# Projected tiles stored through two pairs of buffers in turn, and the upper halves of the last two tiles gated after the third product from the end

## The chip, the core and the metric

The kernel runs on one core of one Trainium2 chip. The core has a matrix engine (PE), a vector engine (DVE), a scalar engine (ACT), a general engine (POOL) and an engine that here issues all the transfers (SP). Each engine runs its own queue of instructions in order and waits on semaphores where it needs what another one makes. The metric is the device time of one execution in microseconds, as the median of several runs.

## The reference

Two branches are computed from the same normalised input, `x` of 2048 positions by 640 features, and multiplied: a dilated sliding window attention (32 heads, 8 places back in steps of 2) with an output projection `wo`, and a bilinear gated unit of 1536 hidden features.

```python
xn = _layernorm(x, axis=-1)
s = _A_ref(xn, A_wqkv, A_wo)                                  # attention(xn) @ wo
g = _silu(_B_ref(xn, B_w_gate, B_w_up, B_w_down))             # ((xn @ w_gate) * (xn @ w_up)) @ w_down
return x + s * g
```

## The kernel before

The 2048 positions are cut into 16 tiles of 128 (`NT`). All numbers are float32; a product is made of three passes of split operands: each operand is written as a high part (rounded, by ACT, the first line of `split`, L85) and a low part (the rest, by DVE or POOL, L86), and `mm3` (L95) adds high by high, high by low and low by high.

The stages follow one another as they are written, since the schedule is by hand: each engine gets its instructions in the order of the program text.

1. Normalisation, the projections to queries, keys and values, and the attention itself, whose vector work is woven in between the products of the gated unit's first half (`gate_up`). `gate_up` makes one chunk of the hidden layer for 512 positions at a time; its result stands in a tile of the pool tag `hs` and is stored to DRAM as `h_scr` (L404). There are 48 such tiles. A scratch tile of tag `gs` holds the gate half (L389), and POOL multiplies the two in the last chunks (L403). Both tags have two buffers, taken in turn.
2. The output projection, a loop over the tiles `s` from 0 to 15 (L766). In each round: `trans_o(s + 1)` transposes the next tile of attention output on DVE (L459) and splits it (L85 on ACT, L86 on DVE); `sum_wd` adds up parts of the down projection's weights on DVE (L507 to L513) from a loaded `wraw` tile; `out_proj(s)` makes two halves of 15 products each on PE into the PSUM tag `q` (4 buffers), evicts each half on ACT into a tile `y` of tag `gs` (L476) and stores `y` to DRAM as `s_scr` (L477); `split_wd` splits the weights (L85 on ACT, L86 on POOL). Tile 14's two split operands are themselves tiles of tag `hs` (L462), since their own tag is by then in use for the next stage.
3. The down projection, in Strassen's manner: 56 products (`n_prod`) of 18 matmuls each (L598), seven for every two tiles. `gather` collects them: of a pair of tiles a and b, the fourth product of the seven completes a's upper half (columns 320 on; L614), the fifth b's upper half (L618), the sixth a's lower half (L621) and the seventh b's lower half; each is then put through silu on ACT (L579). `gated` multiplies by the projected tile (L584), adds the input (L585) and stores to the output (L586); it takes a whole tile or one half. The projected tile and the input are loaded by `load_sx` (L569, L570) into tiles of tags `hs` and `gs`.

Transfers are issued by SP in program order. In the loop over products a pair of tiles is gated in the next pair's first two rounds; only the last pair, tiles 14 and 15, is gated at the end, in the round of product 54 (`m == n_prod - 2`) and after the loop.

Of the kernel before, what the change touches and what calls it, by code (L numbers as in the profile page):

```python
# [19 lines left out]
P = 128  # L20
S, D, F = 2048, 640, 1536
H, DH = 32, 20
W, DIL = 8, 2
NT = S // P
# [6 lines left out]
HALF = D // 2  # L31
# [13 lines left out]
def tile_column(s):  # L45

    return DIL * (s % NE) + s // NE
# [3 lines left out]
def kernel(  # L51
# [23 lines left out]
    def st(shape, tag, bufs, dt=F32):  # L75
        cnt[0] += 1
        return sb.tile(shape, dt, tag=tag, bufs=bufs, name=f"{tag}_{cnt[0]}")

    def pt(shape, tag, bufs):
        cnt[0] += 1  # L80
        return ps.tile(shape, F32, tag=tag, bufs=bufs, name=f"{tag}_{cnt[0]}")
# [8 lines left out]
    def mm3(acc, pairs, parts=ALL3, first=True, last=True):  # L90

        pairs = list(pairs)
        runs = [(a[i], b[j]) for i, j in parts for a, b in pairs]
        for n, (a, b) in enumerate(runs):
            nc.tensor.matmul(acc, a, b, start=first and n == 0, stop=last and n == len(runs) - 1)  # L95
# [372 lines left out]

    def out_proj(s):
        a = oT.pop(s)  # L470
        y = st([P, D], "gs", 2)
        for n in range(2):
            c = slice(n * HALF, (n + 1) * HALF)
            p = pt([P, HALF], "q", 4)
            mm3(p, [([t[:, k, :] for t in a], [t[:, c] for t in wo_s[k]]) for k in range(KD)])
            nc.scalar.activation(y[:, c], p, AF.Copy)  # L476
        nc.sync.dma_start(s_scr[s], y)  # L477
# [60 lines left out]
    def sum_h(m):  # L538

        n, name = m // 7, H_IN[m % 7]  # L540
        v = h_raw[n]
        if name == "S1":
            y = st([P, 2, KH, P], "wqh", 1)
            v["S1"], v["S2"] = y[:, 0], y[:, 1]
            nc.vector.tensor_add(v["S1"], v["A21"], v["A22"])
        elif name == "S2":
            nc.vector.tensor_sub(v["S2"], v["S1"], v["A11"])
        elif name == "S4":
            v["S4"] = st([P, KH, P], "wql", 1)
            nc.vector.tensor_sub(v["S4"], v["A12"], v["S2"])  # L550
        elif name == "S3":
            v["S3"] = v["A21"]
            nc.vector.tensor_sub(v["S3"], v["A11"], v["A21"])

    def hi_h(m):
        hT[m] = st([P, 2, KH, P], "wf", 4, F32R)
        nc.scalar.activation(hT[m][:, 0], h_raw[m // 7][H_IN[m % 7]], AF.Copy)

    def lo_h(m):
        n, name = m // 7, H_IN[m % 7]  # L560
        nc.vector.tensor_sub(hT[m][:, 1], h_raw[n][name], hT[m][:, 0].bitcast(F32))
        if name == "A22" and n + 2 < NT // 2:
            load_h(n + 2)
# [3 lines left out]
    def load_sx(s):  # L567
        a, b = st([P, D], "hs", 2), st([P, D], "gs", 2)
        nc.sync.dma_start(a, s_scr[s])  # L569
        nc.sync.dma_start(b, xv[:, tile_column(s), :])  # L570
        sx_t[s] = a, b
# [9 lines left out]
    def gated(s, half=None):  # L581
        c = slice(0, D) if half is None else slice(half, half + HALF)
        (a, b), y = sx_t[s], g_t[s]
        nc.vector.tensor_mul(y[:, c], y[:, c], a[:, c])  # L584
        nc.vector.tensor_add(y[:, c], y[:, c], b[:, c])  # L585
        nc.sync.dma_start(ov[:, tile_column(s), c], y[:, c])  # L586

    def product(m):
        j = m % 7
        name = W_IN[j]  # L590
        place = "ACACABA"[j]
        new = j in (0, 1, 5)
        if new:
            bank[place] = pt([P, HALF], {"A": "q", "B": "g", "C": "u"}[place], {"A": 4, "B": 2, "C": 2}[place])
        p, y = bank[place], hT.pop(m)
        runs = [(i, l, k) for i, l in ((0, 0), (0, 1), (1, 0)) for k in range(KH)]
        for r, (i, l, k) in enumerate(runs):
            nc.tensor.matmul(p, y[:, i, k], wd_t[name][k][:, l], start=new and r == 0, stop=r == len(runs) - 1,  # L598
                             skip_group_check=True)

    def gather(m):

        n, j = divmod(m, 7)
        a, b = 2 * n, 2 * n + 1
        p = bank["ACACABA"[j]]
        if j == 0:
            keep("M1", p, "lg", 2)
        elif j == 1:
            keep("M5", p, "lg", 2)
        elif j == 2:  # L610
            keep("U2", p, "e", 1)
        elif j == 3:
            g_t[a] = st([P, D], "q", 2)
            nc.vector.tensor_add(g_t[a][:, HALF:], kept["U2"], p)  # L614
            return lambda: silu(a, 1)
        elif j == 4:
            g_t[b] = st([P, D], "q", 2)
            nc.vector.tensor_add(g_t[b][:, HALF:], kept["M5"], p)  # L618
            return lambda: silu(b, 1)
        elif j == 5:  # L620
            nc.vector.tensor_add(g_t[a][:, :HALF], kept["M1"], p)  # L621
            return lambda: silu(a, 0)
        else:
            return lambda: silu(b, 0, p)
        return lambda: None
# [139 lines left out]
    n_prod = 7 * NT // 2  # L765
    for s in range(NT):  # L766
        k, part = divmod(s - 1, 2)
        if s == 1:
            begin_wd()
        if s + 1 < NT:  # L770
            trans_o(s + 1)
        if s in o_next:
            load_o(*o_next[s], st([P, o_next[s][1], D], "t", 2))
        if 0 <= k < KH:
            sum_wd(k, part)
        out_proj(s)
        if 0 <= k < KH:
            split_wd(k, part)
            if part and k + 2 < KH:
                load_wd(k + 2)  # L780
        if s == 12:
            load_h(0)
        if s == 14:
            hi_h(0)
            lo_h(0)
# [9 lines left out]
    for m in range(n_prod):  # L795
        n, j = divmod(m, 7)
        product(m)
        after = gather(m)
        if m + AHEAD < n_prod:
            hi_h(m + AHEAD)  # L800
        after()
        if m + AHEAD + 1 < n_prod:
            sum_h(m + AHEAD + 1)
        if m + AHEAD < n_prod:
            lo_h(m + AHEAD)
        if j < 2 and n:
            gated(2 * n - 2 + j)
            load_sx(2 * n + j)
        if m == n_prod - 2:
            gated(NT - 2)  # L810
            gated(NT - 1, HALF)
    gated(NT - 1, 0)


# [41 lines left out]
```

## Time and profile before

| what | value |
|---|---|
| median of 3 runs | 789.18 us (789.11 to 789.18) |
| profiled execution, its own time | 789.2 us |
| its span, first to last instruction | 787.3 us |
| granted PE clock | 0.999 |
| s_scr stores, issue to landing (min, median, max) | 2.1, 3.6, 8.0 us |
| out stores, issue to landing (min, median, max) | 1.8, 2.4, 4.5 us |

The profile is of one execution. The span is what the hardware profiler recorded on the core, and 1.9 us of the execution's time lie around it. Busy times are sums over an engine's instructions; matmuls overlap, so a row of 15 may be longer than its share of the time. In the waits a row reads: the engine and line that waited, the one that ended the wait, microseconds in total, times, longest. In the timeline a row reads: start, duration, engine, line, operation, what is written and read, and in brackets the idle time before it with what ended it. The chain of waits is followed back from the last instruction, and gives start, duration and engine of each piece.

### The profile page before, as it was taken

The page shows a single profiled execution, that of the slowest core. Times are in us where ns is not written, and L with a number is a line of the kernel's source. Part 1 is how long each engine was busy: PE and PEld are TensorE (multiplying, and loading weights), DVE is VectorE, ACT ScalarE, POOL GpSimd, SP SyncE. Part 2 cuts the span into 40 slices and gives each one's busy share as a digit, 9 for nine tenths or more (in the row PEclk, how much of TensorE's full clock was granted, in tenths as well). Part 3 has the DMA queues.
Part 4 walks back from the last instruction along what each step waited for, and adds up shares of the span by engine and source line. Part 5 has one row for each costly group of instructions (what it writes and reads, how often), then busy time and mean ns, then how long its engine had stood idle before and what let it go on. Part 6 is the DMA issues. An engine that isn't in the chain of part 4 may idle for free. (4 is left out here: it accounts for less than half of the span.)

```text
span 787.3 us, 11221 instructions
## 1 busy us (share of the span) xinstructions
PE 778.0 (99%) x4456; PEld 708.8 (90%) x4456; DVE 658.7 (84%) x658; ACT 234.6 (30%) x536; POOL 147.8 (19%) x110
## 2 busy tenths in 40 slices
PE   8999999999999999999999999999999999999997
PEld 6989898889898888898898989888899999999997
DVE  6889899999999979997999999991277677777775
ACT  5324211121112211311221212113356554444442
POOL 6201212022013200500231000113377600000000
PEclk9999999999999999999999999999999999999999
DMA  8272122141132321404032222322796574555533
GB/s 315 73 229 81 36 69 64 48 123 48 49 94 80 94 71 61 118 27 112 28 118 72 62 82 72 107 87 66 182 258 201 181 262 133 204 200 186 181 101 135
DMA packets 81517, 92.68 MB, mean 118 GB/s; under 512 B 23016, under 2 KB 63032, under 8 KB 81336
## 3 DMA queue, kind: packets, MB, share of 16 engines
q1 hardware_dynamic: 81464, 91.96, 37.7%
q8 instruction: 35, 0.57, 0.3%
q14 instruction: 18, 0.15, 0.1%
HBM read 54.53 MB, written 28.31 MB: 105 GB/s over the span
## 5 line engine op out<-in xcount | busy, mean ns | idle before, releaser
L95 PE MATMUL u<-xc,wf 128*128 128x512 f32 (+1 forms) x735 | 176.2, 390 | 0.0
L95 PE MATMUL g<-xc,wf 128*128 128x512 f32 (+1 forms) x735 | 176.1, 390 | 0.0
L95 PEld LDWEIGHTS u<-xc,wf 128*128 128x128 f32 x735 | 135.7, 187 | 32.2
L95 PEld LDWEIGHTS g<-xc,wf 128*128 128x128 f32 x735 | 135.3, 187 | 31.0
L95 PE MATMUL q<-wqh,xc 128*128 128x300 f32 (+1 forms) x960 | 159.7, 309 | 1.8 <-ACT xc L224 1.0
L95 PEld LDWEIGHTS q<-wqh,xc 128*128 128x128 f32 x960 | 146.0, 188 | 4.3 <-ACT xc L224 1.9
L321 DVE TENSOR_TENSOR t<-q,kv 128x1600 f32<-128x1600 f32 (+1 forms) x48 | 99.3, 2069 | 9.6 <-DMA kv<-kv 9.6
L342 DVE TENSOR_TENSOR t<-e,kv 128x1600 f32<-128x1600 f32 (+1 forms) x48 | 97.5, 2051 | 1.1
L86 POOL TENSOR_TENSOR wf<-wraw,wf 128x256 fp32r<-128x256 f32 (+2 forms) x22 | 47.8, 2197 | 247.6 <-ACT wf L85 229.3
L324 DVE TENSOR_REDUCE lg<-t 128x80 f32<-128x1600 f32 (+1 forms) x48 | 92.6, 1930 | 1.2
L389 ACT ACTIVATE gs<-g 128x512 f32<-128x512 f32 x48 | 28.7, 598 | 205.9 <-PE g L95 197.1
L95 PE MATMUL q<-wql,xc 128*128 128x300 f32 (+1 forms) x480 | 86.0, 309 | 0.0
L350 DVE TENSOR_TENSOR t<-t,t 128x1600 f32<-128x1600 f32 (+1 forms) x36 | 78.0, 2166 | 1.1
L95 PEld LDWEIGHTS q<-wql,xc 128*128 128x128 f32 x480 | 74.3, 188 | 0.0
L289 ACT ACTIVATE kv<-q 128x200 f32<-128x200 f32 (+1 forms) x96 | 33.5, 349 | 133.5 <-PE q L95 133.5
L598 PE MATMUL q<-xc,wf 128*128 128x320 f32 x432 | 67.3, 309 | 0.0
L598 PEld LDWEIGHTS q<-xc,wf 128*128 128x128 f32 x432 | 64.3, 188 | 0.0
L86 POOL TENSOR_TENSOR wql<-wraw,wqh 128x300 fp32r<-128x300 f32 (+4 forms) x15 | 34.2, 2300 | 142.6 <-ACT wqh L85 142.6
L95 PE MATMUL q<-wf,wf 128*128 128x320 f32 x156 | 35.9, 312 | 0.6 <-ACT wf L85 0.6
L400 DVE TENSOR_TENSOR hs<-u,gs 128x512 f32<-128x512 f32 x39 | 26.6, 683 | 0.8 <-issue 0.8
L95 PEld LDWEIGHTS q<-wf,wf 128*128 128x128 f32 x156 | 26.0, 188 | 0.9 <-ACT wf L85 0.8
L86 DVE TENSOR_TENSOR wf<-ot,wf 128x640 fp32r<-128x640 f32 x13 | 13.6, 1045 | 14.1 <-ACT wf L85 14.1
(160 smaller groups left out, 891.4 us busy)
## 6 DMA issues: line engine op xcount, KB each, us to landing
h_scr<-hs SPq DMA_DIRECT2D x48, 256.0 KB, 2.3
wraw<-in_wgu SPq DMA_DIRECT2D x12, 640.0 KB, 4.8
t<-h_scr SPq DMA_DIRECT2D x8, 768.0 KB, 7.4
s_scr<-gs SPq DMA_DIRECT2D x16, 320.0 KB, 3.6
hs<-s_scr SPq DMA_DIRECT2D x16, 320.0 KB, 4.4
gs<-in_x SPq DMA_DIRECT2D x16, 320.0 KB, 4.7
out<-q SPq DMA_DIRECT2D x15, 320.0 KB, 2.5
wraw<-h_scr SPq DMA_DIRECT2D x12, 384.0 KB, 5.7
```

Source lines behind the costliest of these rows:

```text
L86: eng.tensor_sub(lo, raw, hi.bitcast(F32))
L95: nc.tensor.matmul(acc, a, b, start=first and n == 0, stop=last and n == len(runs) - 1)
L289: nc.scalar.activation(kv_t[u][:, :, W - 1 + i, :], p[:, c:].rearrange("p (a c) -> p a c", a=2), AF.Copy)
L321: nc.vector.tensor_mul(t, q.rearrange("p i c -> p (i c)").unsqueeze(1).to_broadcast([P, 2, NE * c]), places(0, j))
L324: nc.vector.tensor_reduce(out=lg[:, :, j:j + 2].rearrange("p n a -> p a n"), in_=heads(t), op=ALU.add, axis=AX.X)
L342: nc.vector.tensor_mul(heads(t), pw, heads(places(1, j)))
L350: nc.vector.tensor_add(acc, acc, t)
L389: nc.scalar.activation(gs, pp[0], AF.Copy)
L400: nc.vector.tensor_mul(hs, pp[1], gs)
L598: nc.tensor.matmul(p, y[:, i, k], wd_t[name][k][:, l], start=new and r == 0, stop=r == len(runs) - 1, skip_group_check=True)
```

## The change

In `out_proj` the tile `y` is taken from tag `hs` for odd tiles 1 to 11, and from `gs` for all the others. In the last rounds of the loop over products, the gating of tiles 14 and 15 is ordered anew: after product 53 the upper halves of both, after product 54 the lower half of tile 14, and after product 55, as before, the lower half of tile 15. Tile 14 is thus gated and stored in two halves and not at once.

```diff
     def out_proj(s):
         a = oT.pop(s)
-        y = st([P, D], "gs", 2)
+        y = st([P, D], "hs" if s % 2 and s < NT - 4 else "gs", 2)
         for n in range(2):
...
         if j < 2 and n:
             gated(2 * n - 2 + j)
             load_sx(2 * n + j)
-        if m == n_prod - 2:
-            gated(NT - 2)
+        if m == n_prod - 3:
+            gated(NT - 2, HALF)
             gated(NT - 1, HALF)
+        elif m == n_prod - 2:
+            gated(NT - 2, 0)
     gated(NT - 1, 0)
```

## The prediction

> **What bounds the kernel now.** I read the busy times, then the waits between the engines, then the timeline wherever TensorE (PE) is not continuous.
>
> ```profile
> span 787.3 us, 11221 instructions
> PE 778.0 (99%) x4456; PEld 708.8 (90%) x4456; DVE 658.7 (84%) x658; ACT 234.6 (30%) x536; POOL 147.8 (19%) x110
> ```
>
> PE is busy for all but 9.3 us, so only a hole in PE, or what runs after the last product, can be won. The change touches two stretches: the output projection (562.8 to 634.5 us: 16 tiles of 30 products, 4.42 us a tile) and the last three products. The waits from 562 to 636 (total, times, longest, us) hold one long wait on ACT and one on PE:
>
> ```profile
> ACT gs L476 <- DMA s_scr<-gs: 3.4, 1, 3.4
> PE q L95 <- ACT wf L85: 0.6, 1, 0.6
> ```
>
> The timeline (start, duration, engine, line) says how they hang together:
>
> ```profile
> 569.25 9.16 SPq L477 DMA_DIRECT2D s_scr<-gs  x3
> 573.22 0.73 ACT L85 ACTIVATE wf<-ot 128x640 fp32r<-128x640 f32 x1
> 577.31 0.77 ACT L476 ACTIVATE gs<-q 128x320 f32<-128x320 f32 x2 [3.36 <-DMA s_scr<-gs]
> 579.40 0.74 ACT L85 ACTIVATE wf<-ot 128x640 fp32r<-128x640 f32 x1
> ...
> 585.65 0.46 PE L95 MATMUL q<-wf,wf 128*128 128x320 f32 x2
> 589.23 0.31 PE L95 MATMUL q<-q,wf 128*128 128x320 f32 x1
> 590.09 0.56 PE L95 MATMUL q<-wf,wf 128*128 128x320 f32 x2 [0.55 <-ACT wf L85]
> ```
>
> Tile 2's eviction (L476) stands at the head of ACT until tile 0's store has left the shared buffer: that store, issued at 569.25, takes 8.0 us to land (landing times by issue window). Every split behind it on ACT (L85) is late, DVE's lower part of tile 4 (L86) waits 2.86 us, and the lag reaches PE at tile 6 through the chain of waits:
>
> ```profile
> 586.20 1.16 DVE wraw L512
> 587.36 1.09 DVE e L513
> 588.45 0.77 DVE ot L459
> 589.30 0.75 ACT wf L85
> 590.09 44.39 PE q L95 x300
> ```
>
> From 590.09 to the last product PE never stops, so what the hole costs is paid at the end in full. The last rows are:
>
> ```profile
> 779.65 0.49 DVE L621 TENSOR_TENSOR q<-lg,g 128x320 f32<-128x320 f32 x1 [2.04 <-PE g L598]
> 780.67 0.82 DVE L584 TENSOR_TENSOR q<-q,hs 128x640 f32<-128x640 f32 x1 [0.54 <-ACT q L579]
> 782.27 0.48 DVE L584 TENSOR_TENSOR q<-q,hs 128x320 f32<-128x320 f32 x1
> 782.28 0.44 ACT L579 ACTIVATE q<-q 128x320 f32<-128x320 f32 x1 [1.64 <-PE q L598]
> 783.20 0.48 DVE L584 TENSOR_TENSOR q<-q,hs 128x320 f32<-128x320 f32 x1
> 784.24 0.33 SPq L586 DMA_DIRECT2D out<-q  x1
> ```
>
> The silu of tile 15's lower half is done at 782.72, but its multiply starts at 783.20: DVE is still busy with tile 15's upper half. DVE, not PE, is last there, by 0.48 us.
>
> **Part one: hs for odd tiles 1 to 11.** No instruction is added and none changes size; buffers and waits change.
> - Removed: tile 2's wait on tile 0's store. It now takes the other gs buffer, whose reader (POOL's L403) ended at 565.0. Tile 4, the next on tile 0's buffer, evicts after 582.6; the store landed at 577.3.
> - Added: tile 1 (evicts at 570.24) and tile 3 (about 578.6) wait for the stores of the last two hs tiles of the gate-and-up stage. These were issued at 558.04 and 566.06 and land after 2.5 and 8.8 us, at 560.5 and 574.9: cost nothing, with 9.7 and 3.7 us of cover. Queued behind tile 1's eviction on ACT are three wd splits and tile 3's split, for which POOL and PE wait; without that cover this is the last rival. Tiles 5 to 11 reuse a buffer four tiles on (17.6 us) against a longest landing of 8.0: nothing.
> - Added: the two hs operands of tile 14 wait for the stores of tiles 9 and 11. Tile 11's is issued by about 617.4 (its second eviction starts at 616.87), so lands at 621.0 by the median of 3.6, before DVE's row at 623.8. Even at 8.0 it lands at 625.4, the lower part is then ready at 626.3, and PE first needs it ten products into tile 14, at 627.0: nothing.
> - SP issues the same stores; tile 2's moves from 578.1 to about 576.6, and the wd and o loads behind it by as much.
>
> Then ACT runs on: tile 2's evictions at 574.0 and 576.2, four wd splits of 0.36 to 578.0, tile 4's split done at 578.7 (580.14 before; PE wants it at 580.4). For tile 5 DVE follows with L86 to 579.5, two wd sums at the slow 1.16, a transpose of 0.83, ACT 0.75: 583.2 against PE's 584.8. For tile 6, L86 to 584.7 (1.48, the slow row), two sums at 1.16, transpose and split: 588.6 against 589.2. So the hole should close. It is worth 590.09 - 589.23 - 0.147 (the usual pitch of products) = 0.71, plus 0.10 (the pair after it, 0.56 for 0.46), plus 0.07 (tile 5's first pair, at 584.85, took 0.53) = **0.88 us**. Bounds: 0, if the slow rows stack up; 0.9, as PE has no other hole here.
>
> **Part two: both upper halves after product 53.** Four DVE rows of 0.49 and two stores now stand ahead of L621. L618 ends at 777.61; tile 14's upper half runs to 778.6 and tile 15's to 779.56, while L621 cannot start before PE ends product 54 (779.65). Their operands are there: tile 15's silu at 778.16, its hs at 777.7, its gs at 773.83 + 4.7 = 778.5. Product 54 hides the 1.95 us; uncovered, they would push L621, which has 1.06 us of slack (below). After L621 come silu (to 780.65) and tile 14's lower half: 2 x 0.49 plus two starts, 781.7 (was 782.35). DVE is then idle until 782.74, two starts of 0.02 after the silu; 0.48 + 0.02 + 0.49 later, at 783.75, SP can issue the last store, not 784.24: **0.49 us**. The split costs DVE 2 x (2 x 0.49 - 0.82) = 0.32 us and SP one more issue of 0.33, all before 782. SP is free: its last earlier issue (773.83, 1.93 us) ends at 775.8, and the four stores go out at about 778.7, 779.6, 781.7 and 783.75, each when its add is done. The last store keeps its 160 KB and its landing, 2.2 us here; the second of the same size landed in 1.8.
>
> **Sum** against the profiled execution: 787.3 - 0.88 - 0.49 = 785.9 us of span, and 789.2 - 1.37 = 787.8 with the 1.9 us around it. The median of the runs is 789.18, so the forecast is the same there: **787.8 us**, 0.17% less. I call 0.2% (1.58 us, so 787.60) the bound, about what a measurement of this kernel can tell from no change.
>
> **The rivals.**
> *The last store is also rid of a fetch: 787.4.* One packet of the instruction queue is in flight around the last store:
>
> ```profile
> q14 instruction: 1, 0.01, 0.8%
> ```
>
> (window 782 to 787.3: packets, MB, share of 16 engines; 0.8% of 16 x 5.3 is 0.7 us on one DMA engine.) The rows of the store are all but through at 785.6, and single packets of one engine trickle to 786.0. That is the 2.2 against 1.8. If the store, half a microsecond earlier, gets clear of it, 0.4 more is won: -1.77. For: the fetch may hang on something that does not move with DVE. Against: it starts shortly after DVE's last row, and may be set off by it. The Trainium skill (DMA: Bandwidth & Descriptors, Queues, rings and completion order) says that a DMA engine takes turns between its queues packet by packet and that one queue is the runtime's own, which fits a single delayed engine; by that rule the sum would be 787.4 if the two miss each other and 787.8 if not.
>
> *The hole stays, only the end is won: 788.7* (789.2 - 0.49). Beside POOL a wd sum takes 1.16, alone 0.48:
>
> ```profile
> 574.99 1.16 DVE L512 TENSOR_TENSOR wraw<-wraw 128x320 f32<-128x320 f32 x1
> 594.74 0.48 DVE L512 TENSOR_TENSOR wraw<-wraw 128x320 f32<-128x320 f32 x1
> ```
>
> POOL also starts earlier, so the two may meet more. I have charged the slow figure throughout and still have 0.6 us at tile 6, so little speaks for it. The Trainium skill (SBUF — State Buffer, Who interferes with whom) has a DVE instruction with two SBUF inputs and a POOL instruction that reads SBUF block one another; if each of the three DVE rows ahead of tile 6 lost a whole POOL row of 1.1, not 0.7, tile 6 would be ready 1.2 us later and the time 788.3 to 788.7.
>
> *Only the hole closes, the end stays: 788.3* (789.2 - 0.88): gs of tile 15 lands over a microsecond later than its 778.5, and holds L621 behind the upper half. This point is past only if L621 starts later than 780.7 instead of 779.65.
>
> *Slower: tile 1 gets the hs buffer of the late store.* It decides if that store lands after 570.24; the one issued at 566.06 does, at 574.9. ACT would then stand for 4.7 us; evictions 0.8, three splits 1.1 and tile 3's split 0.7 put that at 577.5, where PE wants it at 576.0: 1.5 us of hole, a second of up to 1.0 at tile 4 or 5 through DVE, and the old 0.88 kept. With the end's 0.49 off, +1.0 to +2.0: 790.2 to 791.2. Against it: 48 hs tiles came before, an even number, so tile 1 follows the last but one, stored at 558.04.
>
> **How the numbers follow.** Forecast 0.50 (787.55 to 788.1 by itself), the fetch missed 0.34, only the end 0.06, only the hole 0.03, slower 0.07. Faster by over 0.2%: 0.34 and 0.04 from the forecast's lower edge, 0.38; within 0.2%: 0.55; slower: 0.07. The range from 787.2 to 788.9 holds all but the slower case and strays.
>
> **What would show it.** Right: no wait of L476 on s_scr; ACT's split of tile 4 ends near 578.7; no hole near 590, and PE's last product ends at 781.4; the last L584 follows its silu at once, and the last store goes out 1.4 us earlier, at 782.9. Wrong: L476 waiting on h_scr near 570; a new PE wait on L85; L621 starting well after its product; a last landing far from 2.2.

## The result and the profile after

| | before | changed |
|---|---|---|
| median of 14 runs each on one chip | 789.39 us | 787.71 us (787.34 to 788.20) |
| ratio, 95% interval | | 0.9978 (0.9969 to 0.9986) |
| span of the profiled execution | 787.3 us | 785.8 us |
| output projection, start of its first matmul to that of the first product after it | 71.53 us | 70.60 us |
| down projection, start of its first matmul to that of its last | 147.62 us | 147.62 us |
| last silu's start to the end of the span | 5.0 us | 4.2 us |

The forecast was 787.8 us, 1.37 us or 0.17% less than before. The change took off 1.68 us by the medians, 0.21% (0.22% by the ratio of the table). That is just past the bound of 0.2%, with an interval that lies on both sides of it.

The page of the changed kernel begins (span; busy time, share and instructions of each engine):

```profile
span 785.8 us, 11227 instructions
PE 778.8 (99%) x4456; PEld 709.7 (90%) x4456; DVE 659.0 (84%) x660; ACT 234.7 (30%) x536; POOL 147.3 (19%) x110
```

Two more DVE instructions stand there. PE is idle for 7.0 us in place of 9.3. The waits from 562 to 636 us (who, for whom, total, times, longest) have these rows for the evictions, and none for PE (one more of 1.2 us, for which no engine is named, stands in the profile of before as well):

```profile
ACT gs L476 <- PE q L95: 15.1, 11, 1.7
ACT hs L476 <- PE q L95: 8.6, 6, 1.6
```

The evictions of both tags now wait for PE alone, as they should: ACT is ahead. The 3.4 us behind a store are gone. ACT's timeline (start, duration, line; the four weight splits after the third row are left out) shows tile 2's evictions and tile 4's split, and the chain of waits what it does for PE:

```profile
573.65 0.74 ACT L85 ACTIVATE wf<-ot 128x640 fp32r<-128x640 f32 x1
574.33 0.44 ACT L476 ACTIVATE gs<-q 128x320 f32<-128x320 f32 x1
576.47 0.44 ACT L476 ACTIVATE gs<-q 128x320 f32<-128x320 f32 x1 [1.71 <-PE q L95]
578.25 0.73 ACT L85 ACTIVATE wf<-ot 128x640 fp32r<-128x640 f32 x1
```

```profile
563.20 70.60 PE q L95 x480
```

Before, the unbroken piece held 300 products from 590.09 on; now it holds all 480 matmuls of the stage. The split of tile 4 begins at 578.25, not at 579.40. Among the last rows of the timeline are:

```profile
777.77 5.68 SPq L586 DMA_DIRECT2D out<-q  x4
778.18 0.49 DVE L585 TENSOR_TENSOR q<-q,gs 128x320 f32<-128x320 f32 x1
778.97 0.49 DVE L621 TENSOR_TENSOR q<-lg,g 128x320 f32<-128x320 f32 x1 [0.30 <-PE g L598]
781.60 0.44 ACT L579 ACTIVATE q<-q 128x320 f32<-128x320 f32 x1 [1.64 <-PE q L598]
782.07 0.49 DVE L584 TENSOR_TENSOR q<-q,hs 128x320 f32<-128x320 f32 x1 [1.05 <-ACT q L579]
```

DVE is through with the upper halves at 778.67, waits 0.30 us for PE, and after that 1.05 us for the last silu. The last multiply starts 0.47 us after the silu's start; before it was 0.92 (783.20 against 782.28).

The stretches add up to the difference of the spans: 0.93 less in the output projection, 0.79 less at the end, and 0.25 more ahead of both, where nothing was changed (the first matmul of the output projection starts at 563.03, before at 562.78). That start lay between 562.5 and 563.5 in the eight profiles of this study, so it is scatter and no effect.

### The profile page after: what moved, and what is told of

Read it like the earlier page. It is cut to its first block, busy times and chain, and to the rows that moved or that the text cites. A ratio compares the mean times of both kernels' runs of the same rounds, so it can differ in the third digit from the quotient of the medians.

```text
span 785.8 us, 11227 instructions
## 1 busy us (share of the span) xinstructions
PE 778.8 (99%) x4456; PEld 709.7 (90%) x4456; DVE 659.0 (84%) x660; ACT 234.7 (30%) x536; POOL 147.3 (19%) x110
## 4 chain that ended last, share of the span: by engine, by line
PE 99%; DVE 0%; ACT 0%; issue 0%; POOL 0%; POOLq 0%
PE q L95 36%; PE u L95 21%; PE g L95 21%; PE q L598 11%; PE u L598 5%; PE g L598 3%; PE q L157 1%; PE q L223 1%; ACT xc L224 0%; PE q L240 0%; DVE xc L225 0%; DVE q L584 0%; DVE q L585 0%; ACT q L579 0%; POOL ident masks.py:199 0%
## 5 line engine op out<-in xcount | busy, mean ns | idle before, releaser
L321 DVE TENSOR_TENSOR t<-q,kv 128x1600 f32<-128x1600 f32 (+1 forms) x48 | 97.7, 2036 | 10.0 <-DMA kv<-kv 10.0
L350 DVE TENSOR_TENSOR t<-t,t 128x1600 f32<-128x1600 f32 (+1 forms) x36 | 80.3, 2231 | 1.1
```

What stands on the lines that cost most here:

```text
L321: nc.vector.tensor_mul(t, q.rearrange("p i c -> p (i c)").unsqueeze(1).to_broadcast([P, 2, NE * c]), places(0, j))
L350: nc.vector.tensor_add(acc, acc, t)
```

## The experiments

In the diffs below, the kernel changed from is named first. `HS` stands for `"hs" if s % 2 and s < NT - 4 else "gs"`. Times are medians of 11 runs; each comes with its ratio to the kernel before on the same chip, whose median was 789.09 for the first four and 789.15 for the last two.

**The second pair of buffers alone** (from the changed kernel):

```diff
-        if m == n_prod - 3:
-            gated(NT - 2, HALF)
+        if m == n_prod - 2:
+            gated(NT - 2)
             gated(NT - 1, HALF)
-        elif m == n_prod - 2:
-            gated(NT - 2, 0)
```

> The second pair of buffers alone; the end is as it was before. Theory (hole and end are separate terms that add): the hole near 590 closes, L476 waits for no s_scr store, the output projection's 480 products run from 71.7 us to about 70.8, and the time is 0.9 us below before (ratio 0.9989); the last store lands after 2.2 us as in the profile of before. Rival (the end alone carries the gain, and the earlier products only lengthen a wait there): 0 to 0.2 us below before, with the end longer than the 5.0 us it took from the last silu on. If the last store lands after 1.8 us here too, the 0.4 us between the two landings has nothing to do with the new order of the end.

Measured: 788.05 us, ratio 0.9988 (0.9979 to 0.9997), 1.04 us below before. The chain of waits, the timeline and the output stores in a window around the last ones (size, time to landing) read:

```profile
563.38 70.60 PE q L95 x480
```

```profile
781.79 0.44 ACT L579 ACTIVATE q<-q 128x320 f32<-128x320 f32 x1 [1.64 <-PE q L598]
782.71 0.48 DVE L584 TENSOR_TENSOR q<-q,hs 128x320 f32<-128x320 f32 x1
```

```profile
out<-q SPq DMA_DIRECT2D x2, 160.0 KB, 1.8
```

The hole is closed to the same length as in the changed kernel, and the last multiply is as late as before (0.92 us after the silu's start). The last store landed after 1.8 us with the old order, too, not after the expected 2.2, and from the last silu the end took 4.6 us, not 5.0.

**The new order of the end alone** (from the changed kernel):

```diff
-        y = st([P, D], HS, 2)
+        y = st([P, D], "gs", 2)
```

> The new order of the end alone; all projected tiles go through gs as before. Theory: tile 2's eviction again waits 3.4 us for tile 0's store, PE has its hole near 590, and the time is 0.5 us below before if the last store takes 2.2 us to land, 0.9 us if 1.8 us as in the profile of the changed kernel (ratio 0.9994 to 0.9989). Rival (the halves of tile 14 only add work): no change or up to 0.3 us above before, with L621 starting later than 0.1 us after its product.

Measured: 788.73 us, ratio 0.9997 (0.9988 to 1.0005), 0.36 us below before (the quotient of the two medians is 0.9995). By this interval alone it can't be told from no change; the trace shows what it did. Among its waits from 562 to 636 and its last rows are:

```profile
ACT gs L476 <- DMA s_scr<-gs: 3.2, 1, 3.2
PE q L95 <- ACT wf L85: 0.5, 1, 0.5
```

```profile
779.75 0.49 DVE L621 TENSOR_TENSOR q<-lg,g 128x320 f32<-128x320 f32 x1 [0.26 <-PE g L598]
782.39 0.44 ACT L579 ACTIVATE q<-q 128x320 f32<-128x320 f32 x1 [1.64 <-PE q L598]
782.86 0.49 DVE L584 TENSOR_TENSOR q<-q,hs 128x320 f32<-128x320 f32 x1 [1.05 <-ACT q L579]
```

The wait and the hole are back (output projection 71.47 us), and the end is that of the changed kernel, 4.2 us from the silu on. The two parts are separate terms: each stretch is as long as in the changed kernel when its own part is there, whether the other is or not. By the medians 1.04 and 0.36 make 1.40 us. One figure of the expectation was missed: the last store landed after 1.8 us, for which a gain of 0.9 us was expected, and it was 0.36. The 0.9 took the landing of 2.2 us in the one profile of before for the usual one, and in two other profiles with the old order the last store landed after 1.8.

**hs for tile 1 only** (from the changed kernel):

```diff
-        y = st([P, D], HS, 2)
+        y = st([P, D], "hs" if s == 1 else "gs", 2)
```

> As the changed kernel, but hs for tile 1 only, all other tiles in gs. Theory (only tile 2's wait on the one late store ever cost anything): the same time as the changed kernel within 0.2 us, no wait of L476 on a store, no hole of PE. Rival (later stores also hold evictions back, and the second pair is needed to the end): a wait of L476 on s_scr at a later tile, and 0.3 us or more above the changed kernel.

Measured: 787.75 us, ratio 0.9983 (0.9974 to 0.9992): within 0.1 us of the changed kernel. The evictions' waits, besides the same 1.2 us, are:

```profile
ACT gs L476 <- PE q L95: 23.1, 16, 1.7
ACT hs L476 <- PE q L95: 0.7, 1, 0.7
```

No store holds any of them back, and the 480 products again take 70.60 us. One borrowed buffer moves tile 2 off tile 0's, and no later reuse needs the second pair.

**The buffer of the late store** (from the changed kernel), the rival on the slower side:

```diff
-        y = st([P, D], HS, 2)
+        y = st([P, D], "hs" if (s % 2 or s == 0) and s < NT - 4 else "gs", 2)
```

> As the changed kernel, but tile 0 takes hs as well, so that tile 1 gets the hs buffer whose store was issued at 566 and landed only at 575. Theory (the last rival's mechanism, which the even number of earlier hs tiles kept away): tile 1's eviction stands from about 571 to 575, PE has a hole of 1.5 us at tile 3 and up to 1.2 more at tiles 4 and 5, and the time is 1.5 to 2.8 us above the changed kernel (789.2 to 790.5). Rival (the four q banks and the split operands already made carry PE over a wait of 4 us): under 0.5 us above it.

Measured: 790.72 us, ratio 1.0020 (1.0011 to 1.0029): slower than before, and 2.97 us above the kernel with hs for tile 1 only, taken on the same chip. Among the waits from 562 to 636 are:

```profile
ACT hs L476 <- DMA h_scr<-hs: 4.5, 1, 4.5
PE q L95 <- ACT wf L85: 2.2, 3, 1.5
```

The mechanism is as expected and the price is somewhat above the upper figure of 2.8: the output projection takes 73.64 us, 3.05 more than with the hole closed, in three holes before tiles 3, 4 and 5.

**Tile 14 whole** (from the changed kernel):

```diff
         if m == n_prod - 3:
-            gated(NT - 2, HALF)
             gated(NT - 1, HALF)
         elif m == n_prod - 2:
-            gated(NT - 2, 0)
+            gated(NT - 2)
```

> As the changed kernel, but tile 14 is gated whole after product 54 and only tile 15's upper half goes ahead, after product 53: one store and two DVE instructions fewer than in the changed kernel. Theory (only tile 15's upper half ever stood in the way of the last multiply): tile 14's two long rows of 0.82 us end about 0.3 us before the last silu, the last L584 still follows it at once, and the time is that of the changed kernel within 0.2 us. Rival (tile 14's split is what frees DVE): the last L584 starts 0.2 us or more after its silu, and the end from the last matmul's start takes 4.8 us or more, not 4.6. Where the instruction packet falls tells whether it follows the number of instructions: at 2.7 us after the last matmul's start, as with the old order, or at 1.1 us, as with the new one.

Measured: 787.63 us, ratio 0.9981 (0.9972 to 0.9990), the changed kernel within 0.1 us. Among its last rows are:

```profile
780.87 0.83 DVE L585 TENSOR_TENSOR q<-q,gs 128x640 f32<-128x640 f32 x1
781.62 0.44 ACT L579 ACTIVATE q<-q 128x320 f32<-128x320 f32 x1 [1.64 <-PE q L598]
782.08 0.49 DVE L584 TENSOR_TENSOR q<-q,hs 128x320 f32<-128x320 f32 x1 [0.39 <-ACT q L579]
```

With tile 14 in one piece DVE is still done 0.39 us before the last silu's end releases it, and the last multiply follows at once. It takes 4.6 us from the last matmul's start (781.27) to the end. So the split of tile 14 earned nothing; moving tile 15's upper half did it all. The instruction packet began 2.5 us after the last matmul's start, near the old place, and the last store landed after 1.92 us, not 1.78 as in the changed kernel.

**The loads of tiles 5 to 7 later** (from the kernel before):

```diff
-            load_o(5, 3, st([P, 3, D], "t", 2))
         gate_up(f1, ch)
...
         out_proj(s)
+        if s == 0:
+            load_o(5, 3, st([P, 3, D], "t", 2))
         if 0 <= k < KH:
```

> The kernel before, gs alone and the old end, with one thing moved: the four loads of tiles 5 to 7 from o_scr are issued after tile 0's store and no longer ahead of the last h_scr store. Theory (tile 0's store lands after 8 us because it stands behind these loads): it lands in 3 to 5 us, before tile 2's eviction at 574, the wait of 3.4 us and the hole of PE are gone with no second pair of buffers, and the time is 0.9 to 1.0 us below before (ratio 0.9988). Rival (the store is slow for another reason, such as the wd loads beside it): the landing stays over 6 us, the wait over 2 us and the time that of before.

Measured: 788.00 us, ratio 0.9985 (0.9977 to 0.9994), 1.15 us below before. The store of tile 0 in a window at its issue (size, time to landing), and the only row for the evictions among the waits:

```profile
s_scr<-gs SPq DMA_DIRECT2D x1, 320.0 KB, 4.7
```

```profile
ACT gs L476 <- PE q L95: 25.4, 18, 1.7
```

Issued at 567.57 and landed after 4.7 us, the store is out of its buffer before tile 2 needs it. With one pair of buffers and the old end, the 480 products take 70.60 us as well, by the chain of waits:

```profile
562.65 70.60 PE q L95 x480
```

What made the store late was the work queued ahead of it: four loads of 240 KB fewer took 3.3 us off its time to landing, and SP issued it 1.4 us earlier in the stage.

## Why the prediction was right

- *What bounds the kernel.* PE's holes and the end were all there was to win: the product stage took 147.62 us in every one of the eight profiles.
- *The hole, forecast at 0.88 us.* It was 0.93 by the trace (71.53 less 70.60), and 1.04 by the median of the kernel with this part alone. The removed wait and the free buffers of tiles 1 and 3 came as laid out. Both tiles where the lag could have returned had room, though not as reckoned: tile 5's split on ACT was done 1.3 us before PE started that tile (forecast 1.6), tile 6's 1.7 us before (forecast 0.6), since the two sums of weights ahead of it took 0.48 us each and not the slow 1.16 charged for them.
- *The end, forecast at 0.49 us.* DVE's share, the last multiply following its silu, was 0.45 us (0.92 less 0.47). With stores landing after 1.8 us under both orders, the end shrank from 4.92 to 4.59 us, counted from the last matmul's start in the second-pair-alone and the changed kernel: 0.33 us. So the term was mis-sized in what follows the landing, where the prediction had no change. From the last landing to the end of the span it took 0.85 us in the four profiles with three stores at the end (before, second pair alone, tile 14 whole, loads later) and 0.95 us in the four with four stores. Tile 14 whole has the new order for tile 15, so the 0.10 us goes with the split of tile 14, its extra store and two DVE instructions; by what mechanism stays open.
- *The fetch, the rival at 0.34.* The changed kernel's profile does show it: from 5.38 us in the profile of before, the end fell by 0.79, not by 0.33. But the long landing did not come back. In the two other profiles with the old order the packet lies at the same place, 2.75 us after the last matmul's start, took 0.39 us rather than 0.70, and left the store its 1.8. With the new order it lies 1.1 us after the last matmul, clear of the store. So the rival's 0.4 us is not a regular gain of the change. The medians agree: on the same chip, the new order of the end is 0.36 us below the old one with the hole open (the end alone against before), and 0.30 and 0.37 us below it with the hole closed (tile 1 only against the second pair alone; tile 14 whole against the loads later). That is near 0.33 each time, not 0.79, though each interval alone is wide.
- *The rivals in which one part stays.* Neither came. L621 waited for PE by 0.30 us, so tile 15's input was in time.
- *The slower rival.* It is real, and its total came as priced: 1.63 us above the kernel before (790.72 against 789.09), where the prediction had 1.0 to 2.0. Its parts did not. Tiles 3 to 5 lost 3.05 us and not 1.5 to 2.5, and the old 0.88 did not stay beside that, since PE never stops after 588.46 there. The two errors cancel, which is luck. The rival was kept away by the parity of the earlier hs tiles, as the prediction had it.

The mechanism was right. The closeness of the time, 787.71 against 787.8, is in part luck: the kernel before has a median of 789.39 and not 789.18, and the gain was 1.68 and not 1.37 us. The sum of 1.37 us lies inside the interval of the whole change (0.14% to 0.31%, or 1.1 to 2.4 us), and the two single parts make 1.40 by the medians and 1.26 by the traces (0.93 and 0.33). What remains up to 1.68 lies within the interval, and its cause stays open. Whether the change is past the bound of 0.2%, to which the prediction gave 0.38, or within it, 0.55, the measurement does not decide.

## What to carry to other kernels

A wait that costs an off-path engine 3.4 us may cost the bounding engine 0.9, four tiles on: follow the lag through each queue to where the slack runs out, and price the hole there. One late transfer explains one wait, so look for the one buffer or the one transfer ahead of it before adding a pair; one borrowed tile, or four loads issued later, were worth as much here. A buffer borrowed from another stage brings that stage's last store with it, and which of the two stores it is can turn the gain into a loss.

## What was not expected of the hardware

An 8 KB packet of the instruction queue on one DMA engine can hold a 160 KB store back. Where no other store is in flight, the last store's first data goes out 0.83 us after its issue (the four profiles with four stores). In the profile of before the packet ended 1.14 us after the issue, and the last data came 1.81 us after it. With tile 14 whole the packet ended at 0.92 us and the last data came at 1.57. In the six others the packet ended by 0.84 us or before the issue, and the last data came at 1.42 to 1.43 us. In these eight profiles, then, the delay goes with how far the packet reaches past the store's first data and not with its length: with tile 14 whole it took 0.31 us, the least of all eight.

The place of the instruction packet moved by 1.6 us with two DVE instructions and one store more, and by 0.3 us with the new order for tile 15 alone; what sets it off stays open.
